# First layer of a squared-ReLU network: six of nine steps in pairs, 256 tokens to a matmul

## The chip, the cores and the metric

The kernel runs on one core of one Trainium2 chip. The metric is the device time of one execution in microseconds; of several runs the median is given. Each execution is one launch with all inputs in HBM.

## What is computed

```python
# attention: 8 batches x 8 heads, 576 tokens, head size 64, float32
scores = (q @ k.T) / 8
thresh = max(scores, -1) - tau
scores = where(scores >= thresh, scores, -1e9)
attn   = softmax(scores) @ v
# bridge: (B,H,S,D) -> x of 4608 tokens x 512
# network: w_in 512 x 2048, w_out 2048 x 512
h   = maximum(x @ w_in, 0)          # first layer
out = (h * h) @ w_out               # second layer
```

## The kernel before, in words

**Stages.** The attention comes first (to about 512 us) and leaves x transposed in DRAM, as the tiles xT. Then come the first layer (the function `hidden_layer`, nine passes) and the second layer (`output_layer`, nine passes). The 4608 tokens are nine steps of 512, and each pass of either layer is one step.

**Two levels of a seven-product scheme.** Both layers use a Strassen-like scheme with seven products in place of eight, on two levels: 49 products stand for a product of 4 by 4 blocks. The outer index m runs in the order `OUTER` = 1, 2, 6, 7, 4, 5, 3, the inner index k in the order of `inner` = 1, 6, 7, 5, 2, 4, 3. A block here is the seven products of one m. Weights W_IN[m, k], with their sums, lie in SBUF as 128 x 512 tiles. In the first layer a product is four matmuls (line 825), one for each 128 of the 512 columns of W_IN[m, k]; each has 128 weight columns and 128 tokens. In the trace each of these float32 matmuls is two records.

**The operands from x.** A step's x^T is in two parts of the arena (a single SBUF tile): seven places of 512 floats per partition, one for each m, and three further sets, for the inner sums k = 5, 6, 4. `load_x` (line 746) fetches the four raw places m = 1, 7, 2, 3. `prepare_x` (line 774) makes the outer sums (m = 5, 6, 4, and 7 in place) and then the inner sums. In the first layer it makes each of them by `sum_v` (line 762): ACT copies the second operand to a PSUM bank c (line 771), and one turn later DVE adds (lines 122 and 125). `X_AT` gives two such areas: odd steps use one, even steps the other, so that step n + 1 is loaded and summed while step n is multiplied.

**What happens after each product.** `inner` (line 702) calls `tick` after each of the seven products. Engine work is put into the queues in that order, and each engine works its own queue in order. ACT copies the first product of a block to SBUF (line 737, called p1 here). DVE adds the second (u2) and the third (u3) to it, then adds each of the four results; `final` and `add` (lines 837 and 830) let POOL do a second add of 128 x 512. There are six PSUM banks, and the products 5, 6 and 7 of a block accumulate into the banks of the products 1, 3 and 4, so they need p1, u3 and the fourth product's add done. The finished blocks o wait in `squares`; six ticks later ACT applies Relu and Square (lines 804 and 805) and SP stores them to the DRAM tiles gT (line 806), which the second layer loads again.

**The work beside it.** `also` adds to each tick: `chain_out` (line 1098) makes sums of the second layer's weights in 44 chains, each a load from DRAM, four POOL subtractions of 128 x 128 floats at its ticks 6 to 9, and a store at its tick 10; `CHAINS` (line 1052) gives the tick at which each begins. The lines

```python
if 2 <= i <= 5 and at < 6:
    next(xsums)
```

put one half of an x sum (the ACT copy or the DVE add) into each of the first six ticks of the third to the sixth block. The ninth pass makes no x sums; it loads the second layer's first operands and weights.

A tick is written (i, at) below: i is the place of the block in `OUTER`, from 0, and at the product in it, from 0.

Of the kernel before, what the change touches and what calls it, by code (L numbers as in the profile page):

```python
# [48 lines left out]
def kernel(  # L49
# [25 lines left out]
    nc = tc.nc  # L75
    B, H, S, D = q.shape
    P = 128
# [43 lines left out]
    def minus(e, out, x, y):  # L121
        e.tensor_tensor(out=out, in0=x, in1=y, op=ALU.subtract)  # L122
# [622 lines left out]

    def load_x(n, parts=XPARTS):
        at = X_AT[n % 2]
        xo = arena[:, ds(at, 7 * BANK)].rearrange("p (m c t) -> p m c t", m=7, c=2)
        for a, c in parts:
            to = xo[:, AT_B[a][c] - 1, :, :]  # L750

            t0 = n * STEP + c * 2 * NQ
            done = 0
            while done < 2 * NQ:
                b, at = divmod(t0 + done, S)
                m = min(S - at, 2 * NQ - done)
                src = xT[b][ds(a * 2 * P, 2 * P), ds(at, m)].rearrange("(c p) n -> p c n", p=P)
                nc.sync.dma_start(out=to[:, :, ds(done, m)], in_=src)
                done += m
        prepared[n] = (xo, None)  # L760

    def sum_v(op, out, x, y):

        c = b_pool.tile([P, BANK], FP32, tag="b", name="c")
        n = 1
        for m in y.shape[1:]:
            n *= m
        c = c[:, 0:n].rearrange("p (a b) -> p a b", b=y.shape[2])  # L770
        nc.scalar.copy(c, y)  # L771
        return lambda: op(nc.vector, out, x, c)

    def prepare_x(n, add):
# [20 lines left out]
        prepared[n] = of  # L795

    hid = Region(arena, 0, 26 * BANK)
    squares, clock = deque(), {"n": 0}
# [3 lines left out]
    def square(n, j, o):  # L802

        nc.scalar.activation(out=o, in_=o, func=AF.Relu)
        nc.scalar.activation(out=o, in_=o, func=AF.Square)
        nc.sync.dma_start(out=gT[n][j][:, :].rearrange("p (k t) -> p k t", k=4), in_=o)

# [5 lines left out]
    def hidden_layer(n, also):  # L813

        of = prepared.pop(n)
        tile4 = lambda tag, bufs: hid.tile([P, 4, NQ], FP32, tag=tag, bufs=bufs)
# [4 lines left out]
        for m in OUTER:  # L821

            def product(to, k, more):
                for j in range(4):
                    nc.tensor.matmul(  # L825
                        to[:, j, :], W_IN[m, k][:, ts(j, P)], of[k][:, m - 1, :], start=(not more and j == 0), stop=True,
                        skip_group_check=True,
                    )
# [173 lines left out]
    with tc.manual_schedule():  # L1002
# [113 lines left out]

        for n in range(NSTEP):
            last = n == NSTEP - 1
            if not last:
                load_x(n + 1)  # L1120
                xsums = prepare_x(n + 1, sum_v)
            else:
                load_g(0, [(m, k) for m in (7, 4, 1, 2) for k in K_ORDER])
# [21 lines left out]
            hidden_layer(n, also)  # L1145
            if not last:
                next(xsums, None)
        for n in range(NSTEP):
# [75 lines left out]
```

## Time and profile before

| | |
|---|---|
| median of 3 runs | 1308.29 us (1307.66 to 1311.32) |
| the profiled execution, its own time | 1308.12 us |
| its span in the trace | 1306.3 us |
| granted TensorE clock, mean | 0.998 |
| first layer, first to last matmul | 512.3 to 906.2 us |
| PE / weight loads / DVE / ACT / POOL busy | 98% / 89% / 77% / 65% / 70% |

The span runs from the first instruction to the last; the execution's own time has 1.8 us around it. Busy shares are means over three stages with different limits, and a busy PE is one whose records overlap: what a matmul costs is read from the distance of the records.

### The profile page before, as it was taken

What the parts mean: (1) busy time and instruction counts of PE and PEld (TensorE: products, weight loads), DVE (VectorE), ACT (ScalarE), POOL (GpSimd) and SP (SyncE); (2) the same over time, 40 slices, a digit from 0 to 9 for tenths busy, and PEclk for the clock granted to TensorE, in tenths of its full rate; (3) what the DMA queues carried; (4) which work ended last, traced back from release to release, by engine and by line L of the source; (5) the groups of instructions that cost most, each with busy time, mean ns of one, the idle gap of its engine ahead of it and who ended that gap; (6) DMA issues with size and microseconds to landing.
All of it is one profiled execution on the core that took longest, in us unless ns stands there. A gap on an engine that the chain in (4) does not pass through costs nothing.

```text
span 1306.3 us, 47872 instructions
## 1 busy us (share of the span) xinstructions
PE 1284.5 (98%) x19483; PEld 1159.8 (89%) x19483; DVE 1010.8 (77%) x2431; ACT 845.7 (65%) x1498; POOL 916.4 (70%) x1023
## 2 busy tenths in 40 slices
PE   8999999999999999999999999999999999999998
PEld 5777777677777777999999999999999999999998
DVE  5999999999999996877787778777646654665463
ACT  5999999888898985657665766675523432433240
POOL 2777778755555320978897789768777777777775
PEclk9999999999999999999999999999999999999999
DMA  6565666544333313466556665569645234522511
GB/s 153 145 160 140 169 182 188 147 103 104 89 78 79 79 41 80 133 200 218 182 181 194 203 208 164 180 247 393 245 158 162 63 105 158 162 68 96 162 34 33
DMA packets 247035, 192.12 MB, mean 147 GB/s; under 512 B 97184, under 2 KB 195488, under 8 KB 246816
## 3 DMA queue, kind: packets, MB, share of 16 engines
q1 hardware_dynamic: 245504, 188.66, 48.5%
q8 instruction: 153, 2.51, 0.8%
q14 instruction: 66, 0.54, 0.2%
q10 hardware_dynamic: 1312, 0.41, 0.1%
HBM read 116.65 MB, written 72.35 MB: 145 GB/s over the span
## 4 chain that ended last, share of the span: by engine, by line
PE 87%; ACT 5%; DMA 3%; DVE 3%; issue 1%; POOL 1%; SPq 0%; ACTq 0%; DVEq 0%; POOLq 0%
PE po L960 29%; PE ph L825 28%; PE sc L532 11%; PE sc L434 10%; PE pt L380 5%; DVE arena L452 3%; ACT arena L462 2%; PE sc L515 2%; DMA wall<-w 2%; PE sc L398 2%; ACT arena L523 1%; PE sc L380 1%; DMA g<-arena 1%; ACT arena L403 0%; ACT c L771 0%
## 5 line engine op out<-in xcount | busy, mean ns | idle before, releaser
L125 POOL TENSOR_TENSOR arena<-arena 128x512 f32<-128x512 f32 (+1 forms) x314 | 378.1, 1223 | 129.1 <-DVE arena L125 115.1
L960 PE MATMUL po<-wall,arena 128*128 128x128 f32 x3528 | 394.7, 275 | 1.4 <-ACT arena L737 1.4
L960 PEld LDWEIGHTS po<-wall,arena 128*128 128x128 f32 x3528 | 394.3, 192 | 1.8 <-ACT arena L737 1.8
L825 PE MATMUL ph<-arena,wall 128*128 128x128 f32 x3528 | 394.2, 275 | 0.7 <-DVE arena L644 0.7
L825 PEld LDWEIGHTS ph<-arena,wall 128*128 128x128 f32 x3528 | 394.0, 192 | 0.8 <-issue 0.8
L125 DVE TENSOR_TENSOR arena<-ph,arena 128x512 f32<-128x512 f32 x378 | 256.3, 688 | 86.3 <-PE ph L825 63.2
L122 POOL TENSOR_TENSOR arena<-arena 128x128 f32<-128x128 f32 (+2 forms) x314 | 255.4, 814 | 53.8 <-DMA arena<-w 37.6
L125 DVE TENSOR_TENSOR arena<-po,arena 128x128 f32<-128x128 f32 x378 | 108.4, 290 | 168.6 <-PE po L960 164.5
L467 DVE SCALAR_TENSOR_TENSOR arena<-arena 128x576 f32<-128x576 f32 x288 | 237.4, 860 | 1.3 <-POOL arena L459 0.8
L452 DVE TENSOR_SCALAR_CACHE_REDUCE arena<-sc 128x576 f32<-128x576 f32 x288 | 205.0, 747 | 14.6 <-ACT arena L523 4.8
L462 ACT ACTIVATE arena<-arena 128x576 f32<-128x576 f32 x288 | 208.1, 773 | 11.8 <-DVE arena L452 8.5
L771 ACT COPY c<-arena 128x512 f32<-128x512 f32 (+1 forms) x303 | 173.5, 579 | 49.6 <-DVE arena L122 41.7
L532 PEld LDWEIGHTS sc<-arena 64*64 64x64 f32 x5760 | 159.2, 133 | 36.7 <-DVE arena L452 20.2
L532 PE MATMUL sc<-arena 64*64 64x128 f32 (+1 forms) x5760 | 180.8, 262 | 2.7 <-DVE arena L452 1.3
L434 PE MATMUL sc<-arena 64*64 64x64 f32 (+1 forms) x2304 | 176.9, 414 | 6.2 <-ACT arena L403 4.2
L122 DVE TENSOR_TENSOR arena<-arena,c 128x512 f32<-128x512 f32 (+1 forms) x267 | 174.9, 663 | 5.5 <-ACT c L771 4.0
L523 ACT COPY arena<-pt 128x1024 f32<-128x1024 f32 x144 | 146.4, 1017 | 30.5 <-PE pt L380 29.4
L737 ACT COPY arena<-po 128x128 f32<-128x128 f32 x63 | 16.6, 264 | 186.7 <-PE po L960 184.0
L380 PEld LDWEIGHTS pt<-ident,arena 64*128 64x128 f32 x2304 | 83.4, 139 | 39.4 <-ACT arena L523 30.1
L737 ACT COPY arena<-ph 128x512 f32<-128x512 f32 x63 | 36.6, 581 | 123.1 <-PE ph L825 122.5
L434 PEld LDWEIGHTS sc<-arena 64*64 64x64 f32 x2304 | 74.3, 134 | 45.1 <-ACT arena L403 15.1
L380 PE MATMUL pt<-ident,arena 64*128 64x64 f32 x2304 | 102.2, 228 | 2.3 <-ACT arena L523 2.3
(50 smaller groups left out, 922.2 us busy)
## 6 DMA issues: line engine op xcount, KB each, us to landing
g<-arena SPq DMA_DIRECT2D x144, 256.0 KB, 2.6
arena<-g SPq DMA_DIRECT2D x144, 256.0 KB, 4.6
w<-arena SPq DMA_DIRECT2D x60, 256.0 KB, 2.4
wall<-w SPq DMA_DIRECT2D x49, 256.0 KB, 5.2
arena<-w SPq DMA_DIRECT2D x44, 256.0 KB, 3.3
arena<-in_v_dram SPq DMA_DIRECT2D x32, 288.0 KB, 4.0
out_dram<-arena SPq DMA_DIRECT2D x70, 128.0 KB, 2.2
arena<-in_q_dram SPq DMA_DIRECT2D x64, 128.0 KB, 4.0
```

The costliest lines, as they stand in the source:

```text
L122: e.tensor_tensor(out=out, in0=x, in1=y, op=ALU.subtract)
L125: e.tensor_tensor(out=out, in0=x, in1=y, op=ALU.add)
L380: made = nc.tensor.transpose(pt[:, r, ts(slot, HALF)], of[rows, :], ident[rows, rows])
L434: made = nc.tensor.matmul(sc[at, ds(to, count)], lhs, kT[rows, ds(at_k, count)], start=True, stop=True)
L452: made = nc.vector.tensor_scalar(out=s[:, j, :], in0=sc[:, ds(at, S)], scalar1=1.0, scalar2=None, op0=ALU.mult, op1=ALU.min, accum_out=nmx ...
L462: nc.scalar.activation(out=w[:, :, j, :], in_=of(j), func=AF.Exp, bias=nmx[:, j : j + 1], scale=-1.0)
L467: nc.vector.scalar_tensor_tensor(out=w[:, :, j, :], in0=of(j), scalar=thr[:, j : j + 1], in1=w[:, :, j, :], op0=ALU.is_le, op1=ALU.mult, a ...
L523: touch("weights", nc.scalar.copy(joined(to), whole(pt, 0, count)), at, 2 * BANK, m)
L532: made = nc.tensor.matmul(sc[ds(u * D, D), ds(5 * j * BANK + row, count)], loaded_v[i][rows, (c - (u != j)) % CH, :], wT[m][rows, ds(weigh ...
L771: nc.scalar.copy(c, y)
L825: nc.tensor.matmul(to[:, j, :], W_IN[m, k][:, ts(j, P)], of[k][:, m - 1, :], start=(not more and j == 0), stop=True, skip_group_check=True,)
L960: nc.tensor.matmul(to, g[:, j, :], w[:, j, :], start=(not more and j == 0), stop=(j == 3), skip_group_check=True)
```

## The change

Steps 1 and 2, 3 and 4, 5 and 6 are multiplied as pairs. A pair takes two passes; each covers both steps and one half h of the 512 columns of every W_IN[m, k]. A product is then two matmuls, each with 128 weight columns and 256 tokens (128 of each step). Steps 0, 7 and 8 stay as they were. There are nine passes, as before, with 49 products each.

Both areas of x^T hold one pair, so the next pair has no area of its own. Its raw parts are loaded into places as the second pass of the current pair (or pass 0, or pass 6 for the steps 7 and 8) comes to its end with them: m = 1 at tick (1, 0), m = 3 into place 2 at (2, 0), m = 7 into the space of the inner sums at (2, 1), m = 2 at (3, 6), and m = 3 a second time into place 5 at (6, 0) and a third time into place 3 at (0, 0) of the next pass. The sums are put in between by `before_x` and `within_x`; `advance_x` puts one half of a sum into a tick. Outer sums are made for each step, inner sums for both steps and two m at once. The outer sum m = 5 is made by POOL, and the place m = 7 is filled by two ACT copies.

A block o of a pass over a pair is stored by two DMAs, 128 KB each, one to each step's gT. The chains that began at the ticks 0 and 30 of a pass begin 4 ticks before it and at tick 36.

```diff
-    def load_x(n, parts=XPARTS):
+    def load_x(n, parts=XPARTS, slot=None):
...
-            to = xo[:, AT_B[a][c] - 1, :, :]
+            to = xo[:, AT_B[a][c] - 1, :, :] if slot is None else slot
...
+    both = arena[:, ds(X_AT[1], 2 * X_SIZE)].rearrange("p (s z) -> p s z", s=2)
+    places_x = both[:, :, 0 : 7 * BANK].rearrange("p s (m c h t) -> p s m c h t", m=7, c=2, h=2)
+    sums_x = both[:, :, 7 * BANK : X_SIZE].rearrange("p s (k m t) -> p s k m t", k=3, m=7)
+
+    def part_x(steps, k, m, count=None):
+        of = slice((steps[0] + 1) % 2, (steps[0] + 1) % 2 + len(steps))
+        ms = slice(m - 1, m - 1 + count) if count else m - 1
+        if k in (1, 7, 2, 3):
+            return places_x[:, of, ms, k in (2, 3), k in (7, 3), :]
+        return sums_x[:, of, (5, 6, 4).index(k), ms, :]
...
+    def outer_x(steps, op, o, x, y):
+        return [lambda n=n: sum_v(op, slot_x(n, o), slot_x(n, x), slot_x(n, y)) for n in steps]
+
+    def inner_x(steps, m, count=2):
+        of = lambda k: part_x(steps, k, m, count)
+        return [
+            lambda op=op, o=o, x=x, y=y: sum_v(op, of(o), of(x), of(y))
+            for op, o, x, y in ((minus, 5, 7, 1), (minus, 7, 3, 7), (plus, 6, 7, 1), (minus, 4, 2, 6))
+        ]
...
+    BEFORE_X = {(1, 0): (1, 1), (2, 0): (3, 2), (2, 1): (7, None), (3, 6): (2, 2), (6, 0): (3, 5)}
+
+    def before_x(steps, i, at):
+        if (i, at) in BEFORE_X:
+            ask_x(steps, *BEFORE_X[i, at])
...
+        if i == 4 and at < len(steps):
+            nc.scalar.copy(slot_x(steps[at], 7), slot_x(steps[at], 6))
+        work = {
+            (3, 0): lambda: turned_()[0:1], (3, 3): lambda: turned_()[1:],
+            (4, 2): lambda: added()[0:1], (4, 5): lambda: added()[1:],
+            (5, 1): lambda: fourth()[0:1], (5, 4): lambda: fourth()[1:],
+            (5, 6): lambda: inner_x(steps, 1),
+        }
+        return work.get((i, at), list)()
+
+    def within_x(steps, i, at):
+        if (i, at) == (0, 0):
+            ask_x(steps, 3, 3)
+        if (i, at) == (0,1):
+            for n in steps:
+                minus(nc.gpsimd, slot_x(n, 5), slot_x(n, 5), slot_x(n, 6))
+        work = {
+            (0,6): lambda: inner_x(steps, 6),
+            (2,4): lambda: inner_x(steps, 4),
+            (4, 0): lambda: inner_x(steps, 3, 1),
+        }
+        return work.get((i, at), list)()
+
+    def advance_x():
+        if half_made:
+            half_made.pop()()
+        elif waiting:
+            half_made.append(waiting.popleft()())
...
-        nc.sync.dma_start(out=gT[n][j][:, :].rearrange("p (k t) -> p k t", k=4), in_=o)
+        for s_, step in enumerate(steps):
+            nc.sync.dma_start(
+                out=gT[step][j][:, ds(h * BANK // 2, BANK // 2)].rearrange("p (k t) -> p k t", k=2),
+                in_=o.rearrange("p (k s) t -> p k s t", s=2)[:, :, s_, :],
+            )
...
+                if h is not None:
+                    for j in range(2):
+                        nc.tensor.matmul(
+                            to[:, 2 * j : 2 * j + 2, :], W_IN[m, k][:, ts(2 * h + j, P)], part_x(steps, k, m),
+                            start=(not more and j == 0), stop=True, skip_group_check=True,
+                        )
+                    return
...
-        CHAINS = [49 * n + 6 * c for n in range(NSTEP - 1) for c in range(n == 0, 6)][0 : len(chains)]
+        CHAINS = [49 * n + c for n in range(NSTEP - 1) for c in (-4, 6, 12, 18, 24, 36)[n == 0:]][0 : len(chains)]
...
-        for n in range(NSTEP):
+        PASSES = [((0,), None)] + [((n, n + 1), h) for n in (1, 3, 5) for h in range(2)]
+        PASSES += [((n,), None) for n in (7, 8)]
+        for n, (steps, h) in enumerate(PASSES):
             last = n == NSTEP - 1
-            if not last:
-                load_x(n + 1)
-                xsums = prepare_x(n + 1, sum_v)
-            else:
+            group = (n, n + 1) if n == 7 else steps
+            ahead = (n + 1, n + 2) if n in (0, 2, 4, 6) else ()
...
+                if ahead:
+                    waiting.extend(before_x(ahead, i, at))
+                if 0 < n < 8 and h != 1:
+                    waiting.extend(within_x(group, i, at))
+                advance_x()
                 if not last:
-                    if 2 <= i <= 5 and at < 6:
-                        next(xsums)
                     return
```

More of the change, by code (lines that the diff above doesn't have):

```diff
@@ L759, in load_x @@
                 done += m
-        prepared[n] = (xo, None)
+        if slot is None:
+            prepared[n] = (xo, None)
     def sum_v(op, out, x, y):
@@ new lines, in ask_x @@
+    def ask_x(steps, m, slot):
+        (part,) = [(a, c) for a, c in XPARTS if AT_B[a][c] == m]
+        for n in steps:
+            load_x(n, [part], slot_x(n, slot))
+    BEFORE_X = {(1, 0): (1, 1), (2, 0): (3, 2), (2, 1): (7, None), (3, 6): (2, 2), (6, 0): (3, 5)}
+    def before_x(steps, i, at):
+        if (i, at) in BEFORE_X:
+            ask_x(steps, *BEFORE_X[i, at])
+        turned_ = lambda: outer_x(steps, minus, 6, 2, None)
+        added = lambda: outer_x(steps, plus, 6, 6, 1)
+        fourth = lambda: outer_x(steps, minus, 4, 2, 6)
+        if i == 4 and at < len(steps):
[7 more added lines that the diff above has]
+        return work.get((i, at), list)()
@@ L813, in hidden_layer @@
     def hidden_layer(n, also):
-        of = prepared.pop(n)
+        steps, h = n
+        of = prepared.pop(steps[0], None)
         tile4 = lambda tag, bufs: hid.tile([P, 4, NQ], FP32, tag=tag, bufs=bufs)
@@ L1143, in also @@
                     reload(7 * i + at - 10)
-            hidden_layer(n, also)
-            if not last:
-                next(xsums, None)
+            hidden_layer((steps, h), also)
         for n in range(NSTEP):
```

21 lines of the change are left out of this document (19 added, 2 removed).

## The prediction, made before the changed kernel ran

> **What bounds the kernel now.** I read the page first, its busy shares and its slices.
>
> ```profile
> span 1306.3 us, 47872 instructions
> PE 1284.5 (98%) x19483; PEld 1159.8 (89%) x19483; DVE 1010.8 (77%) x2431; ACT 845.7 (65%) x1498; POOL 916.4 (70%) x1023
> PEclk9999999999999999999999999999999999999999
> ```
>
> PE is busy for 98% of the span and its clock is granted in full everywhere. That is a mean over three stages, so the windows of the stage that changes come next: two passes of the first layer and its last.
>
> ```profile
> core 0: us, PE busy (x) PEld busy (x) DVE busy (x) ACT busy (x) POOL busy (x), PEclk, DMA share, GB/s
> 643.70:687.50 43.80, 43.80 (x395) 43.80 (x394) 34.12 (x55) 29.17 (x53) 37.24 (x47) 1.00 0.61 193
> 687.50:731.20 43.70, 43.70 (x393) 43.70 (x393) 34.11 (x55) 29.02 (x53) 36.66 (x46) 1.00 0.61 193
> 862.50:906.30 43.80, 43.80 (x394) 43.80 (x394) 31.46 (x48) 25.99 (x47) 30.09 (x25) 1.00 1.01 369
> ```
>
> In a pass of 43.8 us PE never rests. DVE has 9.7 us to spare, ACT 14.6, POOL 6.6 to 7.1, and the DMA engines are 61% busy. So a pass takes what its matmuls take, as long as no other engine falls so far behind that PE has to wait. Next, the groups of PE by shape.
>
> ```profile
> L825 PE MATMUL ph<-arena,wall 128*128 128x128 f32 x3528 | 394.2, 275 | 0.7 <-DVE arena L644 0.7
> L532 PE MATMUL sc<-arena 64*64 64x128 f32 x4608 | 176.9, 273 | 1.6 <-DVE arena L452 0.2
> L532 PE MATMUL sc<-arena 64*64 64x64 f32 x1152 | 39.7, 220 | 1.1 <-DVE arena L452 1.1
> L434 PE MATMUL sc<-arena 64*64 64x64 f32 x1152 | 34.9, 219 | 0.4 <-ACT arena L403 0.4
> L380 PEld LDWEIGHTS pt<-ident,arena 64*128 64x128 f32 x2304 | 83.4, 139 | 39.4 <-ACT arena L523 30.1
> ```
>
> The layer's 3528 records fill 394.2 us: 111.7 ns from one to the next, and 0.7 us of waiting, all at its first matmul. This 111.7 is the number that the change works on.
>
> **Part 1: the matmuls.** Six passes have 196 matmuls of two records each, 2352 records of 128 tokens; they become 1176 records of 256 tokens. What does a record of 256 take? None is in the trace, so I split the 111.7 into a part that grows with the tokens and a part that doesn't. A record of 128 tokens takes 273 ns from start to end, one of 64 takes 220 or 219: 53 to 54 ns for 64 tokens, so 106 to 108 for 128. That leaves 3.7 to 5.7 ns per record that don't grow. With 4.7, rounded to 5, a record of 256 takes 2 x 111.7 - 5 = 218.4 ns, and the gain is 1176 x 5 = 5.9 us. The bounds: nothing, if the 5 ns is per token after all, and 1176 x 10 = 11.8 us if a long record hides its own 5 ns as well. I take one fixed part per record, since both pairs of rows give one. A product is then four records, 0.873 us, a block 6.11, a pass 42.8.
>
> The Trainium skill, "TensorE: Matmul & The Clock Gate", section Back-to-back issue gap, has two rules for this. One is a table of 134 cycles for 128 columns and 262 for 256, which would make the sum 5.9 us. The other is a sustained spacing of about 81 ns at 128 columns and 131 at 512, set by weight load and matmul together; drawn as a line it gives an estimated 98 ns at 256, 40% less per token, and would make the sum some 100 us. By that rule the trace disagrees: if each record is two passes over its tokens, 111.7 is 56 ns per pass, under its 81.
>
> **Part 2: ACT and DVE, where the x sums now stand.** The counts hardly move: a pair needs 22 ACT copies with 22 DVE adds, and two ACT copies more, where two steps had 24 and 24. The evictions and squares are as many as before, 49 products a pass. What moves is their place. Before, the sums lay in the third to sixth block. Now, in the pass before a pair, they run to its very end: copies at (5, 1), (5, 4), (5, 6), (6, 1), (6, 3), (6, 5), the adds one tick later, and again from (0, 6) to (1, 6) of the next pass. The last two blocks are also where ACT has eight squares, and the next block has four. I work that stretch through by hand, with distances between starts in these rows:
>
> ```profile
> start us, us, engine line op out<-in xcount [idle before <-releaser]
> 657.76 0.60 ACT L771 COPY c<-arena 128x512 f32<-128x512 f32 x1
> 658.28 0.63 ACT L804 ACTIVATE arena<-arena 128x512 f32<-128x512 f32 x1
> ...
> 680.67 1.28 DVE L125 TENSOR_TENSOR arena<-ph,arena 128x512 f32<-128x512 f32 x2
> 681.87 0.55 DVE L122 TENSOR_TENSOR arena<-arena,c 128x384 f32<-128x384 f32 x1
> ...
> 682.67 0.57 ACT L737 COPY arena<-ph 128x512 f32<-128x512 f32 x1
> 683.14 0.63 ACT L804 ACTIVATE arena<-arena 128x512 f32<-128x512 f32 x1
> ...
> 684.34 0.61 ACT L804 ACTIVATE arena<-arena 128x512 f32<-128x512 f32 x1
> 684.99 0.63 ACT L805 ACTIVATE arena<-arena 128x512 f32<-128x512 f32 x1
> 685.52 0.61 ACT L804 ACTIVATE arena<-arena 128x512 f32<-128x512 f32 x1
> ...
> 688.54 0.59 ACT L737 COPY arena<-ph 128x512 f32<-128x512 f32 x1
> ```
>
> So ACT spends 0.52 us on an x copy (657.76 to 658.28), 0.47 on p1 (682.67 to 683.14) and 1.18 on a square (684.34 to 685.52), and DVE 0.60 on an add (two in 1.20), whose end comes 0.08 later. A product can be read 0.2 us after its last record: the pass that begins at 687.5 ends its first product at 688.4, and p1 starts at 688.54.
>
> Time 0 is the start of the block m = 5 of a pair's second pass. ACT's p1 can start at 1.07. From there ACT doesn't rest: two p1 0.94, eight squares 9.44, six x copies 3.12. It reaches the next pass's p1 at 14.57; that product is ready at 12.22 + 1.07 = 13.29. So p1 is 1.3 us late and done at 15.1. The sums themselves are in time: DVE makes k = 6 at about 12.4, needed at 13.09. The last add follows its copy, 14.6 to 15.2; then u2 to 15.8 and u3 to 16.4, visible at 16.5. The product (0, 5) starts at 16.58: 0.1 us to spare.
>
> The next block is tighter. ACT goes on from 15.04: four squares, one bank's copy (0.47) and an x copy: 4.72 + 0.47 + 0.52, so 20.75. There p1 of block 1, ready at 18.33 + 1.07 = 19.40, starts 1.35 late and is done at 21.3. DVE: the x add from 20.8 to 21.4, u2 to 22.0, u3 to 22.6, visible at 22.7, needed at 22.70 by (1, 5). Then another x add to 23.2 and the fourth product's add to 23.8, visible at 23.9, needed at 23.57 by (1, 6): PE waits 0.3 us. After that ACT and DVE catch up, since this block has no squares. I book 0.4 us for each boundary between wide passes (2 to 3, 4 to 5); where one side has narrow products, with blocks of 6.25 us (0 to 1, 6 to 7), 0.3 of it goes, and I book 0.1. That is 1.0 us in all. Bounds: nothing, and three times as much.
>
> **Part 3: POOL.** Two 128 x 512 sums are added at (0, 1) of a pair's first pass, and eight chain subtractions a pass change place.
>
> ```profile
> 683.33 8.70 POOL L125 TENSOR_TENSOR arena<-arena 128x512 f32<-128x512 f32 x7
> L122 POOL TENSOR_TENSOR arena<-arena 128x128 f32<-128x128 f32 x176 | 80.7, 460 | 43.4 <-DMA arena<-w 37.6
> ```
>
> Seven adds take 8.70 us, so the two take 2.5 in a pass that leaves POOL 6.6 us. Behind them wait chain subtractions and the adds of the block m = 2, which begin at (1, 3), 10 us into the pass. POOL's adds of the old pass last until about 692 in the first row, 4.5 us into the new one; with 2.5 and four subtractions of 0.46 it is free by 9. Cost nothing; without that cover it would be up to 2.5 us a pair, 10 in all, through late squares. Moving the chain from tick 30 to 36 takes its four subtractions out of the block m = 5, which already gives POOL six adds; no gain, since PE didn't wait.
>
> **Part 4: transfers and SP.** A pair's blocks are stored as 64 DMAs of 128 KB instead of 32 of 256 KB, in runs of 512 bytes instead of 2 KB, and six raw parts are loaded where four were.
>
> ```profile
> g<-arena SPq DMA_DIRECT2D x144, 256.0 KB, 2.6
> w<-arena SPq DMA_DIRECT2D x60, 256.0 KB, 2.4
> L758 SPq DMA_DIRECT2D arena<-xT x48: 355/420/1950, 300.9 to 821.5; - x48
> DMA to landing us min/median/max: 2.1/3.7/5.6
> ```
>
> The chains' stores w<-arena already go in runs of 512 bytes and land after 2.4 us, the g stores after 2.6: the shorter runs cost no landing time that shows. SP's issues take 0.42 us (the row's median), some 20 more a pass: 8 us of a queue that mostly waits. The DMA engines' share rises from 0.61 to perhaps 0.75 (half as many bytes of x again, g somewhat dearer). The hard date is raw m = 7, loaded into the inner sums' space: it can't be issued before block 1 ends, 12.2 us into the pass, and ACT's copy at (3, 0) wants it at 18.33 + 1.07 + 0.47 = 19.9. It is the third of four loads (1.3 us of issues, then up to 5.6): 19.1. For the steps 5 and 6 all parts are cut in two at a batch's end, and it is the sixth of eight: 12.2 + 2.5 + 3.7 = 18.4 at the median, 20.3 at the maximum. ACT would stand there with DVE's add behind it; no square is due in that block. Cost nothing, with 1 us of cover. The second layer and the last pass keep their instructions.
>
> **Sum.** -5.9 + 1.0 = -4.9 us against the profiled execution's own 1308.12 (span 1306.3, 1.8 around it), which is 0.2 under the median 1308.29. Forecast: 1303.2 us.
>
> **The rivals.**
>
> *The fixed part isn't there* (the change doesn't save what it is for): a record of 256 tokens takes 223.4 ns. For it: my 5 ns is a small difference of rounded rows, and operands that lie in two areas could cost a little. Against it: two rows agree. Then 1308.1 + 1.0 = 1309.1, no change. Chance 0.08.
>
> *ACT's queue costs more*, three times my 1.0 us: 1308.1 - 5.9 + 3.0 = 1305.2, no change. For it: the stretch above has no slack left at three ticks, and a square a little longer than 1.18 us moves all of them. Against it: what is late in it is caught up within a block. Chance 0.19.
>
> *x^T comes late, and the kernel is slower.* Place: ACT's copy of raw 7 at (3, 0) in the four passes that prepare a pair. For it: SP works in order, behind stores that wait for ACT and POOL, and the loads can't be asked earlier. Against it: 61% DMA share, and landings of 5.6 at most. ACT stands, DVE's add behind it, and u3, due at 22.7, goes at 21.9 without it: so PE waits for what the landing, from an issue at 13.5, takes over 7.4 us (copy, add and u3 take 1.8 more). To be slower by 0.3% the four passes must lose 4.9 + 3.9 = 8.8 us, 2.2 each: a landing of over 9.6 us. At 10.4 us it is 3 each: 1303.2 + 12 = 1315.2. Chance 0.17, with the raw 3 and 2 that lie in the same queue.
>
> *The weight load paces the records.* Then a wide record takes only its tokens, 2 x 106 = 212 ns, and the gain is 1176 x 11.4 = 13.4 us: 1308.1 - 13.4 + 1.0 = 1295.7. For it: loads and matmuls have the same distance in this layer. Against it: the loads of 128 columns at L380 fill 83.4 us with 2304, 36 ns each. Chance 0.02. The spacing rule of the Trainium skill's TensorE page, above, would be a stronger form of it.
>
> **How the numbers follow.** 0.3% (3.9 us) is about what a measurement of this kernel tells from no change. The forecast has 0.54 (1301.4 to 1304.4: stalls from 0.2 up to 2 us, a fixed part up to 5.7 ns); no change 0.08 + 0.19, slower 0.17, and 0.02 for the large gain. Faster 0.56, same 0.27, slower 0.17. The range goes from 1301.4 to 1311.0, over the two cases of no change and the beginning of the late x^T; the forecast's own is 1301.4 to 1304.4.
>
> **What would show it.** Right: records of 128x256 at 218 ns distance; the six passes at 42.8 us; PE idle of 0.5 to 2 us in the layer, at the first two blocks of the passes 1, 3, 5 and 7, put down to DVE behind ACT. Wrong: a distance of 223 (first rival); PE idle of over 4 us at those blocks (second); ACT waiting for DMA arena<-xT at the x copies (third); a distance near 212 or less (fourth).

## The result, and the profile after

The changed kernel takes 1305.22 us (median of 14 runs, 1302.32 to 1307.46), the kernel before 1308.61 in the same comparison (14 runs, 1306.54 to 1312.43). The ratio is 0.9971, with a 95% interval of 0.9962 to 0.9981: 3.4 us less, with 2.5 to 5.0 inside the interval. The forecast was 1303.2, or 4.9 us less, in a range of 1301.4 to 1311.0. The measured time lies in that range, but outside the part of it, 1301.4 to 1304.4, that the prediction called the forecast's own.

The page of the changed kernel, the same three rows as before:

```profile
span 1305.4 us, 45865 instructions
PE 1282.6 (98%) x18307; PEld 1120.5 (86%) x18307; DVE 1007.4 (77%) x2423; ACT 844.7 (65%) x1498; POOL 925.0 (71%) x1031
PEclk8999999999999999999999999999999999999999
```

There are 1176 PE records fewer, as the diff says, and 1.9 us less of PE. The profiled execution took 1307.19 us, only 0.93 less than the one before. In it the attention stage, which has no changed line, ended 1.8 us later (the first layer begins at 514.07 us, against 512.28). So the layer is read by itself. The windows below run from its first to its last matmul, first of the kernel before, then of the changed one.

```profile
core 0: us, PE busy (x) PEld busy (x) DVE busy (x) ACT busy (x) POOL busy (x), PEclk, DMA share, GB/s
512.28:906.20 393.92, 393.92 (x3527) 393.92 (x3528) 304.05 (x478) 252.31 (x453) 312.36 (x366) 1.00 0.63 204
```
```profile
514.07:905.33 391.26, 389.55 (x2351) 353.72 (x2352) 300.27 (x470) 250.85 (x453) 321.53 (x374) 1.00 0.72 216
...
600.92:644.09 43.17, 43.03 (x197) 36.98 (x196) 32.34 (x51) 27.42 (x49) 35.78 (x46) 1.00 0.77 215
644.09:688.26 44.17, 43.37 (x197) 36.90 (x196) 35.12 (x57) 30.45 (x57) 40.02 (x49) 1.00 0.71 199
688.26:730.73 42.47, 42.47 (x198) 37.16 (x197) 32.23 (x51) 27.02 (x49) 36.45 (x46) 1.00 0.81 224
730.73:773.96 43.23, 43.03 (x197) 36.98 (x196) 34.93 (x57) 30.33 (x57) 39.05 (x49) 1.00 0.70 195
773.96:816.43 42.47, 42.47 (x198) 37.16 (x197) 32.33 (x51) 27.02 (x49) 35.38 (x45) 1.00 0.75 215
816.43:861.67 45.24, 44.73 (x394) 44.07 (x392) 35.35 (x57) 30.64 (x57) 37.11 (x41) 1.00 0.56 167
```

The layer is 2.66 us shorter; the second layer takes 396.15 us against 395.97, the same. Of the passes over pairs shown here, the two without much waiting (688.26 and 773.96, the passes 4 and 6) take 42.47 us, a little under the 42.8 that was forecast. The first passes of a pair, where new x sums have just been made, take up to 44.17, and the pass after the last pair (816.43 to 861.67), which has narrow products, takes 45.24 instead of 43.7. The DMA share is 0.72 instead of 0.63.

Two numbers say where the 2.66 us come from. The start times of the single records give both. Wide records lie 215.83 ns apart in the mean of those without a wait (190 distances of 215 ns and 954 of 216), narrow ones still 111.67. And all records that come later than that lose 6.2 us in sum, where the layer before lost 0.1. 2352 records at 111.67 less 1176 at 215.83 is 8.8 us of gain; less 6.2 of waits, and with the 0.1 that the layer before lost too, that is the 2.7 measured. (The expectations below were written with 215.7 and 9.0.) The rows of the two shapes, with the mean time of a record from start to end:

```profile
L919 PE MATMUL ph<-arena,wall 128*128 128x256 f32 x1176 | 257.5, 380 | 1.2 <-DVE arena L125 0.5
...
L926 PE MATMUL ph<-arena,wall 128*128 128x128 f32 x1176 | 132.7, 275 | 1.2 <-DVE arena L644 0.7 <-DVE arena L125 0.5
```

The waits of the weight loads, in the passes 1 to 7, with lines of two other engines that the next paragraphs use (columns: total us, times, longest):

```profile
POOL arena L122 <- DMA arena<-w: 6.8, 8, 1.8
PEld ph L919 <- DVE arena L125: 6.2, 14, 0.9
ACT arena L888 <- POOL arena L125: 5.4, 6, 1.5
...
PEld ph L926 <- DVE arena L125: 1.1, 3, 0.7
...
PEld ph L919 <- ACT arena L737: 0.5, 1, 0.5
```

PE's waits are waits for DVE's u2, u3 and adds, as was forecast, and in one case for ACT's p1: 18 waits here, and 19 places by the records' starts. Most are at the products (0, 5), (1, 5) and (1, 6) of the passes 1, 3, 5 and 7; the largest are at (1, 5) of pass 3 (0.67 us) and of pass 7 (0.64). How pass 3 comes to it shows in the timelines of POOL, ACT and PE around the boundary at 644.09:

```profile
630.60 0.46 POOL L122 TENSOR_TENSOR arena<-arena 128x128 f32<-128x128 f32 x1
632.19 0.46 POOL L122 TENSOR_TENSOR arena<-arena 128x128 f32<-128x128 f32 x1 [1.12 <-DMA arena<-w]
632.60 1.28 POOL L125 TENSOR_TENSOR arena<-arena 128x512 f32<-128x512 f32 x1
```
```profile
647.87 0.63 ACT L888 ACTIVATE arena<-arena 128x512 f32<-128x512 f32 x1 [0.82 <-POOL arena L125]
...
653.62 0.58 ACT L737 COPY arena<-ph 128x512 f32<-128x512 f32 x1
```
```profile
655.88 0.48 PE L919 MATMUL ph<-arena,wall 128*128 128x256 f32 x1 [0.50 <-DVE arena L125]
```

POOL, late in pass 2, stands 1.12 us for a chain's load. SP issued this load at 628.17, after it had stood 2.7 us for the store of an earlier chain to land, not behind other issues. The kernel before has the same wait of POOL at this place (1.09 us, up to 630.38), and it cost nothing there. Here POOL works without rest from 632.19 to 653.2, with a chain's subtractions among its last adds, so the adds slip; ACT stands 0.82 us for one of them at 647.05. ACT's queue has no rest in this stretch, so the p1 of block 1 is that much late (653.62), DVE's u3 behind it too, and PE stands. The last row is the first record after that wait, 0.67 us late by its start: it takes 0.48 us where the mean is 0.38, and the next one starts 0.32 us after it instead of 0.216. Each of the 19 places of the layer where PE waited shows this second loss of 0.10 us, together 2.0 of the 6.2 us.

### The profile page after: what moved, and what is told of

It reads as the page before. It is cut to its first block, busy times and chain, and to the rows that moved or that the text cites. A ratio compares the mean times of both kernels' runs of the same rounds, so it can differ in the third digit from the quotient of the medians.

```text
span 1305.4 us, 45865 instructions
## 1 busy us (share of the span) xinstructions
PE 1282.6 (98%) x18307; PEld 1120.5 (86%) x18307; DVE 1007.4 (77%) x2423; ACT 844.7 (65%) x1498; POOL 925.0 (71%) x1031
## 4 chain that ended last, share of the span: by engine, by line
PE 83%; ACT 6%; DMA 4%; DVE 4%; issue 2%; POOL 1%; SPq 0%; DVEq 0%; ACTq 0%; POOLq 0%
PE po L1061 29%; PE ph L919 16%; PE sc L532 11%; PE sc L434 10%; PE ph L926 8%; PE pt L380 5%; DVE arena L452 3%; DMA wall<-w 2%; ACT arena L462 2%; PE sc L515 2%; PE sc L398 2%; ACT arena L523 1%; ACT arena L888 1%; DMA g<-arena 1%; PE sc L380 1%
## 5 line engine op out<-in xcount | busy, mean ns | idle before, releaser
L122 POOL TENSOR_TENSOR arena<-arena 128x128 f32<-128x128 f32 (+1 forms) x322 | 264.8, 824 | 23.1 <-DMA arena<-w 6.8
L919 PE MATMUL ph<-arena,wall 128*128 128x256 f32 x1176 | 257.5, 380 | 1.2 <-DVE arena L125 0.5
L919 PEld LDWEIGHTS ph<-arena,wall 128*128 128x128 f32 x1176 | 222.1, 190 | 36.3 <-DVE arena L125 6.2
L776 ACT COPY c<-arena 128x512 f32<-128x512 f32 (+1 forms) x295 | 168.6, 578 | 76.9 <-DVE arena L125 37.8
L122 DVE TENSOR_TENSOR arena<-arena,c 128x512 f32<-128x512 f32 x235 | 154.3, 666 | 15.7 <-ACT c L776 13.2
L926 PE MATMUL ph<-arena,wall 128*128 128x128 f32 x1176 | 132.7, 275 | 1.2 <-DVE arena L644 0.7
L926 PEld LDWEIGHTS ph<-arena,wall 128*128 128x128 f32 x1176 | 131.8, 192 | 2.1 <-DVE arena L125 1.1
```

What stands on the lines that cost most here:

```text
L919: nc.tensor.matmul(to[:, 2 * j : 2 * j + 2, :], W_IN[m, k][:, ts(2 * h + j, P)], part_x(steps, k, m), start=(not more and j == 0), stop=Tr ...
L926: nc.tensor.matmul(to[:, j, :], W_IN[m, k][:, ts(j, P)], x, start=(not more and j == 0), stop=True, skip_group_check=True,)
```

## The experiments

In all of them, "layer" is the time from its first to its last matmul in the run's profile, and "waits" is the sum by which records of the layer start later than 215.8 or 111.7 ns after the one before. For the changed kernel the layer is 391.3 with waits of 6.2, for the kernel before 393.9 with 0.1. Ratios are against the kernel before in the same comparison.

### The width alone, and the sums alone

The first takes out the x sums of the second and third pair and of the steps 7 and 8; loads, chains and stores stay.

```diff
-        if i == 4 and at < len(steps):
+        if i == 4 and at < len(steps) and steps[0] == 1:
-        if (i, at) == (0,1):
+        if (i, at) == (0,1) and steps[0] == 1:
+                if n > 1:
+                    waiting.clear()
```

> The changed kernel with the x sums of the pairs 3+4, 5+6 and of the steps 7 and 8 left out (ACT copies, DVE adds and POOL adds; the raw parts are still loaded, and the matmuls multiply what lies in the places). The sums of the pair 1+2 stay. In the changed kernel's trace PE waits 6.2 us in the first layer (first to last matmul 391.3 us), nearly all in the first two blocks of the passes 1, 3, 5 and 7. Theory (the sums at the pass boundary overfill ACT's and DVE's queues): the waits of the passes 2 to 7 go, 5.5 us, those of pass 1 (0.7) stay; the layer takes 385.8 to 387 us, the kernel 4.5 to 5.5 us less than the changed one. Rival A (transfers: shorter stores, more loads of x, SP): the transfers are all there, so the waits stay and the layer takes about 391. Rival B (POOL, with the chains' subtractions in front of the last adds): two POOL adds a pair less, little changes, about 390.5.

Measured: 1301.43 us, ratio 0.995 (0.9935 to 0.9965), layer 387.2, waits 2.1. Of PE's waits for DVE this is left in the passes 1 to 7:

```profile
PEld ph L919 <- DVE arena L125: 3.0, 7, 0.6
```

So 4.1 us of the waits hang on the sums: the prediction's mechanism, and about four times its price. POOL's two adds for m = 5 are left out too, so the 4.1 isn't shown to be ACT's and DVE's alone.

The second makes four matmuls of 128 tokens of each wide product again and leaves everything else as changed.

```diff
-                    for j in range(2):
+                    for j in range(4):
-                            to[:, 2 * j : 2 * j + 2, :], W_IN[m, k][:, ts(2 * h + j, P)], part_x(steps, k, m),
+                            to[:, j, :], W_IN[m, k][:, ts(2 * h + j // 2, P)], part_x(steps, k, m)[:, j % 2, :],
```

> The changed kernel with its pairs, sums, stores and chains, but each product of a pair as four matmuls of 128 tokens, as before the change (each weight tile of 128 columns used twice in a row). Theory (the width is the whole gain: 215.7 ns for a record of 256 tokens against 2 x 111.7): records again 111.7 ns apart, 9.0 us more of them; blocks of 6.25 us give ACT and DVE 0.14 us more each, so the waits at the boundaries fall from 6.2 to about 3; the layer takes 391.3 + 9.0 - 3 = 397 us, the kernel 5 to 6.5 us more than the changed one and about 2 to 3 more than before the change. Rival (the order of the work or the same weights twice in a row give the gain, not the width): the layer stays near 391 to 393.

Measured: 1309.37 us, ratio 1.0011 (1.0001 to 1.002), layer 396.3, waits 2.5. The group of the pairs' matmuls:

```profile
L919 PE MATMUL ph<-arena,wall 128*128 128x128 f32 x2352 | 264.3, 275 | 0.6 <-DVE arena L125 0.5
```

Without the width the rest of the change costs 2.4 us in the layer, all of it waits; with the width the layer is 5.1 us shorter than this, 8.8 less 3.7 of further waits. A pass of narrow records takes 43.8 us (392 x 111.67) without waits, one of wide records 42.3 (196 x 215.83). The same work of ACT and DVE has 1.5 us less, and more than half of the waits come with that.

### POOL and the place of the chains

The third leaves the chains' subtractions out; their loads and stores stay.

```diff
-                    minus(nc.gpsimd, t[:, to, :], t[:, x, :], t[:, y, :])
+                    pass
```

> The changed kernel without the POOL subtractions of the weight chains (their loads and stores stay; the sums of the second layer's weights are left out). Theory (ACT and DVE queues at the boundaries; POOL only adds to it in the passes 3 and 7, where ACT waits for POOL's last adds): the extra waits of the passes 3 and 7, about 0.9 and 0.6 us, go, the rest stays; the layer takes 389.5 to 390.2 us. Rival B (POOL is the cause): the waits fall to under 1.5 us, the layer takes about 386.5.

Measured: 1302.21 us, ratio 0.9957 (0.9942 to 0.9972), layer 388.8, waits 3.8:

```profile
PEld ph L919 <- DVE arena L125: 4.8, 12, 0.5
```

POOL's work on the chains, with its waits for their loads, is worth 2.5 us of the layer, more than the 1.5 expected and less than the rival's share. The gain lies in the passes 2, 3 and 7 (0.7, 0.9 and 0.9 us); the passes 1 and 5 keep their 0.7 and 0.9, so there the sums in ACT's and DVE's queues are enough. The prediction had booked nothing for POOL. The 2.5 and the 4.1 of the first run overlap: together they are more than the 6.2 that there is.

The seventh run puts the chains back to the ticks of the kernel before and keeps all else changed.

```diff
-        CHAINS = [49 * n + c for n in range(NSTEP - 1) for c in (-4, 6, 12, 18, 24, 36)[n == 0:]][0 : len(chains)]
+        CHAINS = [49 * n + 6 * c for n in range(NSTEP - 1) for c in range(n == 0, 6)][0 : len(chains)]
```

> The changed kernel with the chains at the ticks of the kernel before (0 and 30 in place of -4 and 36). Theory: at 30 four subtractions of 0.53 us stand among POOL's six adds of the block m = 5, and at 0 four more behind the two new POOL sums; ACT's last squares and the adds of m = 2 come 1 to 2 us later at each boundary to a pair; the waits rise from 6.2 to 8 to 10 us, the layer takes 393 to 395 us, the kernel 2 to 4 us more than the changed one. Rival (the place of the chains is of no weight, as the prediction had it): 391.3 within 0.5.

Measured: 1314.17 us, ratio 1.0047 (1.003 to 1.0064), layer 401.3, waits 16.3. The expected size was 2 to 4 us; it is 10. Its waits in the passes 1 to 7, and POOL and ACT at the boundary from pass 2 to 3:

```profile
POOL arena L122 <- DMA arena<-w: 14.6, 12, 2.1
...
ACT arena L888 <- POOL arena L125: 12.1, 17, 1.4
DVE arena L125 <- POOL arena L125: 11.9, 13, 1.8
...
ACT c L776 <- DMA arena<-xT: 5.9, 5, 2.3
```
```profile
641.60 8.66 POOL L125 TENSOR_TENSOR arena<-arena 128x512 f32<-128x512 f32 x7
650.23 2.50 POOL L122 TENSOR_TENSOR arena<-arena 128x512 f32<-128x512 f32 x2
```
```profile
645.37 0.63 ACT L888 ACTIVATE arena<-arena 128x512 f32<-128x512 f32 x1 [1.17 <-POOL arena L125]
```

With four subtractions in the block m = 5, POOL's last seven adds run to 650.2, and only then come the two adds of the outer sum m = 5. ACT's squares stand for the adds one after the other (12.1 us in 17 waits, where the changed kernel has 5.4 in 6). The place of the two moved chains of a pass, which cost nothing in the kernel before, is worth more than the width's net gain here; what each of the two costs wasn't separated.

POOL isn't the whole of it. The last waits in the first view are ACT's for x^T, which the changed kernel doesn't have. SP stands longer for chains' stores to land, with the loads of x^T behind it in its queue:

```profile
SPq L1211 <- DMA w<-arena: 57.2, 21, 4.2
```

In the changed kernel that row is 25.5 us in 15 waits. Behind the late copies, DVE's adds and u3 come late, and PE waits at (3, 5) of the passes 2, 4 and 6 (1.6, 0.9 and 0.3 us): some 3 of the 16.3 us. That is the prediction's third rival, in its place and by its path, though not in the changed kernel itself.

### Other orders of the sums

The fourth moves one batch of inner sums, those of m = 6, from (0, 6) to (1, 0).

```diff
-            (0,6): lambda: inner_x(steps, 6),
+            (1, 0): lambda: inner_x(steps, 6),
```

> The changed kernel with the inner sums of m = 6 and 7 begun at tick (1, 0) in place of (0, 6), so that ACT's copy p1 of the block m = 2 and DVE's u2 stand ahead of the first of them. Theory: by the prediction's working u3 and the fourth product's add of that block come 0.6 us earlier; the waits at (1, 4) to (1, 6), 3.75 us over the four boundaries, fall to 1 to 1.5; those at (0, 5) stay; the layer takes 388.8 to 389.5 us, the kernel 2 to 2.5 us less than the changed one. Rivals A and B: no change, 391. Should the sums come too late for the block m = 6, new waits appear at (2, 1) to (2, 5).

Measured: 1303.97 us, ratio 0.9967 (0.9954 to 0.9979), layer 390.9, waits 5.8. A miss: the waits at (1, 4) to (1, 6) go, but for those at (1, 5) of the passes 3 and 7, and PE now stands 0.6 us at (2, 1) at every boundary. That product needs the sum k = 6 of m = 6, which has become the late one. Most of the waits were moved, not removed.

The fifth makes the sum k = 6 second (as 3 - 5), and starts the last sum of the batch m = 1 and the batch m = 6 later.

```diff
-            for op, o, x, y in ((minus, 5, 7, 1), (minus, 7, 3, 7), (plus, 6, 7, 1), (minus, 4, 2, 6))
+            for op, o, x, y in ((minus, 5, 7, 1), (minus, 6, 3, 5), (minus, 7, 3, 7), (minus, 4, 2, 6))
-            (5, 6): lambda: inner_x(steps, 1),
+            (5, 6): lambda: inner_x(steps, 1)[0:3],
-            (0,6): lambda: inner_x(steps, 6),
+            (0, 1): lambda: inner_x(steps, 1)[3:], (1, 0): lambda: inner_x(steps, 6),
```

> The changed kernel with three moves of x sums: the inner sums of m = 6 and 7 begin at tick (1, 0) in place of (0, 6); the sum k = 6 is made second, as 3 - 5 in place of 7 + 1 (so that it is there for the second product of its block); the last inner sum of m = 1 and 2 (k = 4) has its ACT copy at (0, 1), behind the next pass's p1, in place of (6, 5). Theory: the waits at (0, 5) and at (1, 4) to (1, 6) that ACT's and DVE's queues cause go, 0.4 and 0.5 us for each of the four boundaries; what POOL's late adds cause in the passes 2, 3 and 7 stays, 2 to 2.5 us; the layer takes 387.3 to 388 us (changed kernel 391.3), the kernel 3 to 4 us less than the changed one. Rival (the sums fit nowhere, the waits only move): new waits at (2, 1) or (2, 2) as with the later start alone; the layer takes 389.5 us or more.

Measured: 1301.41 us, ratio 0.9954 (0.9939 to 0.9969), layer 389.6, waits 4.5. By medians that beats both kernels, but the layer gains only 1.7 us, where 3 to 4 were expected: a miss. The waits in block 1 shrink; those at (0, 5) grow to between 0.4 and 0.6 us, and the profile now puts them down to DVE's line 122, the sum k = 4 that this product reads:

```profile
PEld ph L919 <- DVE arena L125: 2.4, 7, 0.6
PEld ph L919 <- DVE arena L122: 2.4, 3, 0.9
```

The sixth adds other chain ticks to the fifth: seven chains in a pair's first pass and four in its second (five in pass 0).

```diff
+        CHAINS = [49 * n + c for n in range(NSTEP - 1) for c in ((0, 6, 12, 18, 24, 30, 36) if n % 2 else (6, 13, 20, 27, 34)[0 : 4 + (n == 0)])][0 : len(chains)]
```

> As the run with the sums reordered, and the weight chains moved out of the way: the passes that prepare a pair (0, 2, 4, 6) begin four chains (pass 0 five) at the ticks 6, 13, 20, 27 (34), the others seven at 0 to 36. Theory: with no chain subtractions in the last two blocks before a pair, POOL's adds for the squares are in time, and the waits of the passes 2, 3, 6 and 7 go; waits in the layer under 1 us, the layer takes 385.5 to 386.3 us, the kernel 1.3 to 2.5 us less than with the reordering alone. Rival (POOL isn't what is late there): as the reordering alone. Rival (POOL is overfilled in the passes that now have seven chains): new waits in the first blocks of the passes 2, 4 and 6.

Measured: 1305.40 us, ratio 0.9983 (0.9971 to 0.9995), layer 392.1, waits 7.1: a miss, as 386 was expected. The passes 3 and 7 lose less (0.8 and 0.6 us), but the passes 2, 4 and 6 now lose 2.3, 1.0 and 1.0, after passes in which POOL had seven chains:

```profile
ACT arena L888 <- POOL arena L125: 9.8, 9, 2.2
```

The ninth takes the last sum of the batch m = 1 off ACT: DVE subtracts it from SBUF directly. The sum k = 6 is second and the batch m = 6 starts at (1, 0), as in the fifth run.

```diff
-            (5, 6): lambda: inner_x(steps, 1),
+            (5, 6): lambda: inner_x(steps, 1)[0:3] + [lambda: lambda: minus(nc.vector, *(part_x(steps, k, 1, 2) for k in (4, 2, 6)))],
```

> The changed kernel with the inner sums of m = 6 and 7 begun at (1, 0), k = 6 made second as 3 - 5, and the last inner sum of m = 1 and 2 (k = 4, at (6, 6)) made by DVE straight from SBUF, with no ACT copy. Theory: ACT comes to the next pass's p1 0.5 us earlier and DVE needn't wait for that copy, so the waits at (0, 5), 0.4 to 0.7 us a boundary in the run with the sums reordered, go; the late POOL adds in the passes 2, 3 and 7 stay, about 2 us; the layer takes 387 to 388 us (389.6 with the sums reordered, 391.3 changed), the kernel about 1300. Rival: DVE's add of two SBUF operands is slow beside POOL's (1.2 us or more instead of 0.66), and the waits at (0, 5) stay; the layer takes 389 us or more.

Measured: 1301.49 us, ratio 0.9944 (0.9928 to 0.9959), layer 388.7, waits 3.6, of which 1.0 at (1, 5) of pass 3, the place that was traced to POOL above. Its layer is the shortest of the kernels that leave nothing out, though 387 to 388 were expected; by medians it stands level with the fifth, and it beats both kernels too.

### The stores

These four change the kernel before. The eighth stores each block by two DMAs, in runs of 512 bytes on both sides, in all nine passes. (The changed kernel's split stores have runs of 512 bytes in SBUF and of 1 KB in DRAM.)

```diff
-        nc.sync.dma_start(out=gT[n][j][:, :].rearrange("p (k t) -> p k t", k=4), in_=o)
+        to = gT[n][j][:, :].rearrange("p (k s t) -> p k s t", k=2, s=2)
+        for s_ in range(2):
+            nc.sync.dma_start(out=to[:, :, s_, :], in_=o.rearrange("p (k s) t -> p k s t", s=2)[:, :, s_, :])
```

> The kernel before the change with each block of the first layer stored by two DMAs of 128 KB in runs of 512 bytes, as the changed kernel stores a pair's blocks. Theory and prediction (the stores are covered): the layer stays at 393.9 us, within 0.5, and the kernel within 1 us. Rival A (SP's issues and the shorter runs delay what stands behind them, chains above all): PE waits of over 1 us appear in the layer, 395 us or more.

Measured: 1328.67 us, ratio 1.0164 (1.0149 to 1.018), layer 402.2, waits 8.4; the second layer 407.8, 11.8 more than before, and no run shows why. The first layer was expected to stay at 393.9. Waits in the passes 1 to 7, then SP's issues and POOL's adds in pass 2:

```profile
POOL arena L122 <- DMA arena<-w: 53.8, 18, 7.2
ACT arena L804 <- POOL arena L125: 20.1, 25, 1.4
DVE arena L125 <- POOL arena L125: 17.8, 12, 1.8
```
```profile
599.51 5.18 SPq L808 DMA_DIRECT2D g<-arena  x8
604.79 3.14 SPq L758 DMA_DIRECT2D arena<-xT  x6
607.98 0.46 SPq L1112 DMA_DIRECT2D arena<-w  x1
```
```profile
613.47 2.06 POOL L122 TENSOR_TENSOR arena<-arena 128x128 f32<-128x128 f32 x4 [7.21 <-DMA arena<-w]
```

POOL is idle from 606.26, and SP comes to issue the load it needs at 607.98, behind eight stores and six loads of x^T: 8.3 us of nothing but issuing. After that POOL's adds come late, ACT's squares and DVE behind them. These stores cost SP 610 ns each at the median; the changed kernel's cost 476, the old ones 320:

```profile
L808 SPq DMA_DIRECT2D g<-arena x288: 512/610/1822, 527.3 to 941.8; - x144
```
```profile
L895 SPq DMA_DIRECT2D g<-arena x192: 359/476/1546, 573.6 to 828.5; - x192
```

Two runs take this apart. The tenth keeps one DMA a block and gives the tiles of the steps 1 to 6 gaps, so that it writes runs of 512 bytes (the second layer reads them so). The eleventh keeps long runs and stores the steps 1 to 6 by two DMAs.

```diff
+    wide_g = lambda n: BANK + 128 * (1 <= n <= 6)
+    gT = [[dram.tile([P, wide_g(n)], FP32, name=f"g{n}_{j}") for j in range(16)] for n in range(NSTEP)]
+        nc.sync.dma_start(out=gT[n][j][:, :].rearrange("p (k t) -> p k t", k=4)[:, :, 0:NQ], in_=o)
```

> The kernel before the change with the blocks of the steps 1 to 6 stored by one DMA each, as before, but in four runs of 512 bytes per partition (rows of gT with gaps; the second layer's loads of these steps go in such runs too). In the run with split stores the first layer took 402.2 us against 393.9. Theory (SP's queue: twice as many issues hold up the chains' loads behind them): no more issues here, so the layer stays at 393.9, within 1 us. Rival (the short runs make the transfers slow): the layer takes 398 us or more. The second layer may become slower by its loads; that decides nothing.

Measured: 1311.98 us, ratio 1.0025 (1.0016 to 1.0035), layer 393.9, no waits in it; the second layer, which loads the short runs, 400.6 (4.6 more). The Trainium skill, "Perfetto Trace Analysis", section DMA Optimizations, says that DMAs under 2 KB have a significant overhead per transfer. That is about whole transfers; these are of 256 KB, and only their runs are short, so no run here tests it. The short runs cost the stage that reads them 4.6 us, and the one that writes them nothing.

```diff
+        for a in range(2):
+            nc.sync.dma_start(out=to[:, 2 * a : 2 * a + 2, :], in_=o[:, 2 * a : 2 * a + 2, :])
```

> The kernel before the change with the blocks of the steps 1 to 6 stored by two DMAs each, in runs of 1 KB (half of the columns each). Theory (SP's queue): the waits of the passes 2 to 7 come as in the run with split stores, 5 to 8 us; the layer takes 399 to 402 us. Rival (short runs): runs of 1 KB cost little, the layer takes 394 to 395.5 us.

Measured: 1309.07 us, ratio 0.9999 (0.9989 to 1.0009), layer 393.9, no waits, though POOL waits as long for its chain loads as in the kernel before, or longer (37.6 there):

```profile
POOL arena L122 <- DMA arena<-w: 40.3, 9, 6.2
```

The theory that twice the issues decide fell: 428 ns an issue here, about 22.5 us of issuing in each of the passes 2 to 6, cost nothing. The last run puts the changed kernel's chain ticks under the eighth's stores.

```diff
+        CHAINS = [49 * n + c for n in range(NSTEP - 1) for c in (-4, 6, 12, 18, 24, 36)[n == 0:]][0 : len(chains)]
```

> The kernel before the change with all blocks of the first layer stored by two DMAs of 128 KB in runs of 512 bytes, as in the run with split stores (first layer 402.2 us against 393.9, PE waits 8.4 us), and with the chains at the changed kernel's ticks (-4 and 36 in place of 0 and 30). Theory (the split stores put the chains' loads late on SP, POOL stands before its adds, ACT before its squares; the changed ticks take the chains out of that place): the waits fall to under 2 us, the first layer takes 394 to 396 us. Rival (the split stores cost by themselves, wherever the chains are): 400 us or more. What the last pass's split stores cost the second layer stays in both.

Measured: 1332.29 us, ratio 1.0179 (1.0161 to 1.0197), layer 404.7, waits 10.8. That fell too. POOL waits less for loads and ACT still stands for POOL:

```profile
POOL arena L122 <- DMA arena<-w: 32.5, 13, 5.5
...
ACT arena L804 <- POOL arena L125: 22.6, 21, 2.2
```

So the stores are harmless at some 22.5 us of issuing in a pass (eleventh), and at 27.5 to 29.4 us (eighth) they aren't. The changed kernel lies between, with 23 to 28. But single passes don't follow such a limit: pass 4 of the changed kernel, with the most issuing (27.6 us), loses 0.2 us and pass 3, with 23.7, loses 1.9; in the eighth run pass 1 loses 0.3 us with 28.1 of issuing and pass 2 loses 2.8 with 29.4. What stands in the queue, and when, seems to matter more than the sum; that is argued, not shown. Why the new ticks help in the one kernel and not in the other stays open.

## Why the prediction was right, and where it was off

**The forecast's direction and range held; its two terms were both too small, and in part they cancel.** It had -5.9 + 1.0 = -4.9 us; the layer shows -8.8 + 6.2, which with unrounded terms is -2.7. That the sum came out as near as it did is luck: the one term was short by 2.9 us and the other by 5.2.

**Part 1, the matmuls.** The mechanism is right: the second run shows that without the width there is no gain. The term mis-sized is the fixed part of a record: 7.5 ns are saved by joining two (2 x 111.67 - 215.83), not 5. The prediction took 106 to 108 ns for the part that grows with 128 tokens, from rows of other matmuls (64 x 64) rounded to a nanosecond; the layer's own rows, 275 and 380 ns, give 105, and the distances 104.2. The fourth rival, loads that pace the records, wanted 212 or less, and PE's loads are now busy for less time than its matmuls (36.98 us against 43.03 in pass 2). The Trainium skill, "TensorE: Matmul & The Clock Gate", section Back-to-back issue gap, has 134 cycles for 128 columns and 518 for 512; two 128s and one 512 of it, at 2.4 GHz, are an estimated 111.7 and 215.8 ns. These agree with the trace's 111.67 and 215.83, but only if the narrow record is counted as two runs over its tokens and the wide one as a single run over twice as many. No one way of counting fits both: the 262 cycles that the same table has for 256, taken twice, give an estimated 218.3 ns for the wide record, and taken once 109.2 for the narrow one. So the agreement explains nothing yet. The sustained spacing of that section isn't seen here.

**Part 2, ACT and DVE.** The working by hand named the places: (0, 5) with nothing to spare, (1, 5) on the edge, (1, 6) late. PE waits there, for DVE, in the passes 1, 3, 5 and 7. The wait at (1, 6), forecast at 0.3 us, is 0.2 in each of the four. But the size in all was wrong by a factor of five to six: 5.0 us in the first two blocks of these passes (0.7, 1.9, 0.9 and 1.5) and 6.2 in the layer, instead of 1.0. Three things were left out. Each wait costs the record after it 0.10 us more (2.0 us in 19 places). The narrow neighbours don't save the boundaries 0 to 1 and 6 to 7 (0.7 and 1.5 us in the passes 1 and 7, booked 0.1 each). And the stretch was worked out with POOL on time.

**Part 3, POOL.** "Cost nothing" and "no gain" for the moved chain are the steps that failed. POOL's chain work costs 2.5 us (third run), since ACT's squares stand for its adds in the very stretch where ACT has no rest. What the two new sums at (0, 1) cost by themselves no run shows. And the two moved chains of a pass together are worth 10 us in this kernel (seventh run): "since PE didn't wait" was true of the kernel before only.

**Part 4, transfers and SP.** In the changed kernel x^T was never late: its loads land after 4.0 us at the median and 5.8 at most, and no copy waits for one. That hangs on the place of the chains: in the seventh run five copies wait. The DMA share of 0.75 came (0.70 to 0.81 in the passes 2 to 6). Chain loads came late to POOL (6.8 us of waits in the passes 1 to 7, less than the 37.6 before, but now where POOL has no rest behind them), which the prediction didn't look at: its part on SP asked only for the x^T loads behind the stores. An issue of a split store takes 476 ns where it took 420. Whether "cost nothing" holds for the split stores in the changed kernel no run shows, since none changes its stores alone; it fails by 8.3 us in the kernel before, in the dearer form of the eighth run.

**The rivals.** The nearest is the second, ACT's queue, which was said to show by PE idle of over 4 us at those blocks: it did, with 5.0, and the 6.2 us of the whole layer are twice its price. Its time, 1305.2 us, is the measured one, but by luck too: its sum has 5.9 and 3.0 where 8.8 and 6.2 stand. That the result lies below no change is owed to the width, which gave 2.9 us more than booked. The first and the fourth rival fell with the distance of 215.8 ns, which is neither 223 nor 212; the third didn't come in this kernel.

## What to carry to other kernels

When two engines' queues are nearly without rest at the end of a stage, a third engine's small delay goes straight through them to the engine that bounds the kernel, and work that cost nothing there must be priced again: ask who issues its loads, and what that queue waits for before it comes to them. Count a wait of PE with the 0.10 us that the next record loses, and count waits by places, since each short one pays it. A sum that is moved a few ticks moves the wait with it; only less work on the busy engine, or an order that has the needed sum first, took waits away.

## What was unexpected of the hardware

In the profile the wide record after a wait takes 0.48 us instead of 0.38, and the one behind it starts 0.10 us late, after waits of 0.06 us as after those of 0.67. The time of a DMA's issue on SP goes with the form of its addresses, and with what stands right before it. The medians are 320 ns for a block in one piece, 428 for half a block in runs of 1 KB, 476 for half a block in runs of 512 bytes in SBUF and 1 KB in DRAM, and 610 where both sides have runs of 512. The shortest are 319, 319, 359 and 512, so the 428 isn't the form: of these half blocks, the 55 issues that begin at least 0.2 us after the end of the one before take 320 at the median, and the 137 right behind another 439. Two joined records of 128 tokens save 7.5 ns.
